# A written-out order of the first operations replaced by another, with other filler transposes

## The chip, the cores and the metric

The kernel runs on one core of a Trainium2 chip. Its time is the device time of one execution in microseconds; three runs before the change gave 608.42, 608.91 and 609.12, median 608.91. PE is the matrix engine, DVE the vector engine, ACT the scalar engine, POOL the general engine; SP issues nearly all DMAs. All five work from their own queues, strictly in order, and wait for each other by semaphores.

## What is computed

Lightning attention over 4 batches, 8 heads, 768 tokens and 64 columns a head, in blocks of 64 tokens with a running state, followed by two matrix products with a leaky ReLU between them:

```python
for b in range(nb):
    qb, kb, vb = (q[:, :, sl], k[:, :, sl], v[:, :, sl])
    intra = np.einsum('bhic,bhjc->bhij', qb, kb) * Dmask[None]
    intra = np.einsum('bhij,bhjd->bhid', intra, vb)
    inter = np.einsum('bhid,bhde->bhie', qb * lam_pow[None], kv_state)
    out[:, :, sl] = intra + inter
    kb_dec = kb * rev_pow[None]
    kv_state = lam_block[None, :, None, None] * kv_state + np.einsum('bhsd,bhse->bhde', kb_dec, vb)
...
x = attn_out.transpose(0, 2, 1, 3).reshape(B * S, H * D)      # 3072 x 512
h = x @ w_in                                                  # 512 x 2048, float64
g = np.maximum(0.01 * h, h)
return (g @ w_out).astype(np.float32)                         # 2048 x 512, float64
```

## The kernel before, in words

**Chunks and groups.** Tokens are taken in 24 chunks of 128 (two blocks of the reference at a time), six to a batch. Four chunks make a token group of 512; there are six groups. For every chunk PE transposes k and q (four 128x128 transposes each, line 546), forms the product of decayed k with v that updates the state ("k*v", line 410 in function kv), the scores (line 410 in go; DVE multiplies them by the mask, line 637), and the output of the chunk: first the own part, then two parts with the state (line 410 in own and inter). Between the two state parts a two-column copy (line 676) makes PE wait for the first to be written. Copies of the transposed k and q are line 527, the decay of k line 585, the scaled q line 592, the state update lines 642, 644 and 647.

**Splitting.** The products that follow need more than one pass's precision, so each operand is kept as three tiles: h (line 692 on ACT), l (line 700 on DVE) and m (line 718 on DVE) of the chunk's output x; and likewise wh, wl, wm of a weight slice (lines 806 or 808, 811, 817). Weights come as 64-bit floats, half a slice to a DMA (line 781), and are first turned into 32-bit floats by three ACT operations (793, 795, 797) and two DVE operations (799, 800).

**The first product, "up" (line 853).** For a group and one of eight weight slices, PE makes two blocks, each of four h, four l and four m matmuls into one PSUM bank; between l and m ACT scales the bank (line 878), and at the end ACT applies the leaky ReLU (line 881) and a DMA stores the block (884). Slices 1 of group 0 are done in two halves of two chunks, the 128x256 matmuls of the profile. An up of a group needs the h, l and m of all its chunks. The two buffers of x serve the groups in turn (group number modulo 2).

**The second product, "down" (line 920).** After all ups, from about 341 us on, PE does nothing but this until the end.

**What sets the order.** The program's operations are numbered as the code adds them, each with an engine (or several that could do it), a duration as its author guessed it, and what it reads and writes. The class Plan fixes their order in two stages (method emit). First comes the list ORDER, line 268, written out by hand or by a search: pairs of an operation's number and its engine. A negative number -n does not stand for an operation: it puts n filler transposes of the identity on PE (function busy, line 346, into a free PSUM bank), which compute nothing that is used. What the list leaves out is then placed by a greedy planner: of all operations that are able to run, the one that could start earliest by the guessed durations, ties by a rank that follows the list seq (line 961). The instructions are written out in the order that results; each engine, and SP's DMA queue, receives its own in that order. Nine more fillers come before everything (WARM). Which PSUM bank, raw buffer or store buffer an operation uses is also decided as it is placed.

The loads at the start that both orders move: k and q of a chunk are two DMAs of 128 KB each (line 466), v is one of 256 KB (line 524), half a weight slice one of 512 KB (line 781). Below, k0, q0, v0 stand for those of chunk 0, w10 and w11 for the halves of weight slice 1, w00 and w01 for those of slice 0. Before, SP's queue begins k0 q0 v0 w11 k1 v1 q1 k2 w10 q2 v2 k3 q3 v3 w01 w00.

Of the kernel before, what the change touches and what calls it, by code (L numbers as in the profile page):

```python
# [241 lines left out]
def kernel(  # L242
# [22 lines left out]
    T = GC * C  # L265
    WARM = 9
    LATER = 2.0
    ORDER = [(3, "DMA"), (4, "DMA"), (-6, "PE"), (6, "PE"), (8, "ACT"), (7, "PE"), (5, "DMA"), (9, "ACT"), (0, "DVE"), (1, "DVE"), (10, "POOL"), (13, "PE"), (2, "DVE"), (11, "DVE"), (15, "DVE"), (12, "PE"), (14, "DVE"), (-1, "PE"), (19, "PE"), (20, "PE"), (16, "POOL"), (17, "DVE"), (21, "DVE"), (101, "DMA"), (26, "DMA"), (29, "PE"), (33, "DVE"), (22, "PE"), (28, "DMA"), (36, "PE"), (18, "POOL"), (38, "DVE"), (39, "POOL"), (103, "ACT"), (23, "ACT"), (24, "DVE"), (27, "DMA"), (31, "ACT"), (102, "ACT"), (30, "PE"), (32, "ACT"), (-1, "PE"), (35, "PE"), (37, "DVE"), (40, "DVE"), (41, "POOL"), (34, "DVE"), (105, "DVE"), (49, "DMA"), (95, "DMA"), (96, "ACT"), (104, "ACT"), (52, "PE"), (56, "DVE"), (42, "PE"), (43, "PE"), (97, "ACT"), (50, "DMA"), (-1, "PE"), (53, "PE"), (98, "ACT"), (54, "ACT"), (55, "ACT"), (44, "DVE"), (25, "DVE"), (106, "DVE"), (99, "DVE"), (51, "DMA"), (-2, "PE"), (59, "PE"), (45, "PE"), (61, "DVE"), (100, "DVE"), (72, "DMA"), (73, "DMA"), (46, "ACT"), (75, "PE"), (107, "ACT"), (58, "PE"), (57, "DVE"), (47, "DVE"), (60, "DVE"), (76, "PE"), (155, "PE"), (74, "DMA"), (179, "DMA"), (78, "ACT"), (62, "POOL"), (79, "POOL"), (108, "DVE"), (63, "DVE"), (77, "ACT"), (173, "DMA"), (80, "DVE"), (48, "DVE"), (65, "PE"), (66, "PE"), (67, "ACT"), (-2, "PE"), (68, "PE"), (156, "PE"), (-1, "PE"), (81, "PE"), (180, "ACT"), (69, "ACT"), (70, "DVE"), (64, "POOL"), (84, "DVE"), (85, "POOL"), (181, "ACT"), (182, "ACT"), (174, "ACT"), (175, "ACT"), (82, "PE"), (83, "DVE"), (157, "PE"), (158, "PE"), (120, "DMA"), (111, "DMA"), (110, "DMA"), (119, "DMA"), (112, "DMA"), (88, "PE"), (89, "PE"), (114, "PE"), (159, "ACT"), (90, "ACT"), (91, "PE"), (176, "ACT"), (92, "ACT"), (183, "DVE"), (109, "DVE"), (160, "PE"), (123, "PE"), (86, "DVE"), (177, "DVE"), (184, "DVE"), (93, "DVE"), (178, "DVE"), (-1, "PE"), (164, "PE"), (113, "PE"), (165, "PE"), (161, "PE"), (217, "DMA"), (211, "DMA"), (136, "DMA"), (117, "DVE"), (116, "ACT"), (125, "ACT"), (115, "ACT"), (128, "PE"), (129, "PE"), (135, "DMA"), (121, "DMA"), (185, "ACT"), (71, "DVE"), (127, "DVE"), (186, "DVE"), (122, "PE"), (219, "ACT"), (124, "ACT"), (162, "ACT"), (166, "PE"), (241, "PE"), (167, "PE"), (242, "PE"), (138, "PE"), (87, "POOL"), (94, "DVE"), (118, "DVE"), (218, "ACT"), (213, "ACT"), (214, "ACT"), (212, "ACT"), (221, "DVE"), (131, "DVE"), (130, "DVE"), (-1, "PE"), (137, "PE"), (139, "PE"), (140, "PE"), (232, "DMA"), (132, "POOL"), (126, "DVE"), (133, "DVE"), (134, "POOL"), (220, "ACT"), (142, "PE"), (143, "PE"), (215, "DVE"), (222, "DVE"), (141, "ACT"), (243, "ACT"), (168, "ACT"), (144, "PE"), (145, "ACT"), (149, "ACT"), (148, "ACT"), (246, "PE"), (247, "PE"), (169, "PE"), (187, "DVE"), (216, "DVE"), (223, "ACT"), (244, "PE"), (170, "PE"), (234, "ACT"), (248, "ACT"), (151, "DVE"), (224, "DVE"), (153, "DVE"), (189, "DMA"), (226, "DMA"), (163, "DMA"), (188, "DMA"), (154, "DMA"), (275, "DMA"), (252, "PE"), (253, "PE"), (171, "ACT"), (233, "ACT"), (228, "ACT"), (227, "ACT"), (235, "ACT"), (249, "PE"), (191, "PE"), (152, "DVE"), (146, "DVE"), (190, "PE"), (150, "POOL"), (225, "DVE"), (229, "ACT"), (236, "DVE"), (230, "DVE"), (231, "DVE"), (192, "PE"), (193, "PE"), (194, "DVE"), (195, "PE"), (196, "PE"), (197, "PE"), (245, "ACT"), (202, "ACT"), (250, "ACT"), (237, "DVE"), (238, "DVE"), (206, "DVE"), (239, "DVE"), (254, "ACT"), (201, "ACT"), (277, "PE"), (320, "DMA"), (322, "ACT"), (288, "ACT"), (198, "ACT"), (321, "ACT"), (257, "PE"), (258, "PE"), (255, "PE"), (172, "DMA"), (326, "DMA"), (327, "ACT"), (204, "DVE"), (324, "DVE"), (207, "POOL"), (208, "DVE"), (203, "POOL"), (328, "ACT"), (259, "ACT"), (323, "ACT"), (330, "DVE"), (205, "DVE"), (199, "DVE"), (325, "DVE"), (329, "ACT"), (331, "DVE"), (332, "DVE"), (333, "DVE"), (268, "PE"), (269, "PE"), (263, "PE"), (256, "ACT"), (260, "PE"), (352, "DMA"), (274, "DMA"), (354, "ACT"), (210, "DMA"), (276, "PE"), (278, "PE"), (279, "PE"), (298, "DMA"), (281, "PE"), (282, "PE"), (355, "ACT"), (280, "ACT"), (261, "ACT"), (283, "PE"), (300, "PE"), (340, "PE"), (264, "PE"), (284, "ACT"), (311, "ACT"), (346, "DMA"), (251, "DMA"), (289, "POOL"), (209, "POOL"), (292, "DVE"), (293, "POOL"), (353, "ACT"), (265, "ACT"), (291, "DVE"), (446, "DVE"), (335, "PE"), (341, "PE"), (287, "ACT"), (348, "ACT"), (336, "PE"), (349, "ACT"), (270, "ACT"), (347, "ACT"), (356, "DVE"), (240, "DVE"), (266, "PE"), (267, "ACT"), (285, "DVE"), (271, "PE"), (272, "ACT"), (337, "ACT"), (296, "DMA"), (297, "DMA"), (299, "PE"), (301, "PE"), (302, "PE"), (303, "ACT"), (262, "DMA"), (411, "DMA"), (405, "DMA"), (294, "DVE"), (463, "DVE"), (334, "DVE"), (471, "DMA"), (458, "DMA"), (477, "DMA"), (455, "DMA"), (350, "DVE"), (357, "DVE"), (304, "PE"), (305, "PE"), (351, "DVE"), (306, "PE"), (338, "PE"), (358, "ACT"), (310, "ACT"), (307, "ACT"), (359, "DVE"), (308, "DVE"), (286, "DVE"), (309, "DVE"), (450, "DMA"), (273, "DMA"), (339, "ACT"), (342, "ACT"), (413, "ACT"), (407, "ACT"), (406, "ACT"), (388, "PE"), (361, "PE"), (343, "PE"), (362, "PE"), (344, "ACT"), (383, "PE"), (384, "PE"), (389, "PE"), (479, "DMA"), (454, "DMA"), (319, "DMA"), (470, "DMA"), (478, "DMA"), (447, "DMA"), (457, "DMA"), (366, "PE"), (367, "PE"), (360, "DVE"), (314, "DVE"), (200, "DVE"), (295, "POOL"), (412, "ACT"), (415, "DVE"), (147, "DVE"), (385, "ACT"), (390, "ACT"), (414, "ACT"), (408, "ACT"), (368, "ACT"), (391, "PE"), (386, "PE"), (369, "PE"), (468, "DMA"), (345, "DMA"), (472, "DMA"), (431, "DMA"), (437, "DMA"), (451, "DMA"), (464, "DMA"), (363, "ACT"), (364, "PE"), (365, "ACT"), (387, "ACT"), (370, "ACT"), (371, "DMA"), (459, "DMA"), (448, "DMA"), (449, "DMA"), (313, "POOL"), (290, "POOL"), (409, "DVE"), (315, "DVE"), (316, "POOL"), (317, "DVE"), (416, "DVE"), (494, "PE"), (495, "PE"), (312, "POOL"), (497, "PE"), (498, "PE"), (496, "DVE"), (499, "PE"), (410, "DVE"), (417, "DVE"), (461, "DMA"), (453, "DMA"), (462, "DMA"), (456, "DMA"), (503, "DVE"), (392, "ACT"), (452, "DMA"), (460, "DMA"), (393, "DMA"), (418, "DVE"), (432, "ACT"), (435, "DVE"), (433, "ACT"), (434, "ACT"), (436, "DVE"), (394, "PE"), (395, "PE"), (396, "ACT"), (439, "ACT"), (399, "PE"), (440, "ACT"), (372, "PE"), (425, "PE"), (373, "PE"), (438, "ACT"), (374, "ACT"), (465, "DMA"), (474, "DMA"), (400, "PE"), (401, "ACT"), (397, "PE"), (426, "PE"), (402, "PE"), (513, "DVE"), (441, "DVE"), (419, "DVE"), (442, "DVE"), (443, "DVE"), (510, "DVE"), (475, "DMA"), (398, "ACT"), (403, "ACT"), (512, "DMA"), (404, "DMA"), (480, "DVE"), (522, "DVE"), (377, "PE"), (375, "PE"), (376, "ACT"), (427, "ACT"), (555, "PE"), (378, "PE"), (379, "ACT"), (476, "DMA"), (469, "DMA"), (420, "PE"), (421, "PE"), (422, "ACT"), (380, "PE"), (556, "PE"), (381, "ACT"), (423, "PE"), (428, "PE"), (444, "DVE"), (467, "DMA"), (529, "DMA"), (473, "DMA"), (525, "DMA"), (561, "DMA"), (445, "DVE")]
    APART = 4
    FIRST_LOADS = ["k0", "q0", "v0", "k1", "q1", "v1", "w10", "k2", "q2", "v2", "w11", "k3", "q3", "v3"]  # L270
    LOW_PE, MIX_PE = set(), set()
# [772 lines left out]
```

## Time and profile before

| what | value |
|---|---|
| three runs, us | 608.42, 608.91, 609.12 |
| profiled execution: span from first to last instruction, us | 606.1 (its own total time is not shown; the median of the runs is 2.8 above the span) |
| PE busy, us and share of the span | 595.4, 98% |
| DVE, ACT, POOL busy, us | 308.5, 266.9, 73.4 |
| PE busy in 0 to 20 and 20 to 40 us | 14.74 and 18.10 |
| mean busy share of the DMA engines, 0 to 40 us | 92 to 93% |
| filler transposes (line 349) | 25: 9 at the start, 16 from the list |
| one 512-column matmul of line 853, start to start, four in a row | 0.91 us for four |

In rows of the timeline the first number is the start in us from the span's start, the second the length; then engine, line, operation, output and inputs, their shapes and how many were merged; in brackets how long the engine had been idle and what ended that. In the table by windows, each engine's busy time and number of instructions stand in the order PE, PEld (weight loads), DVE, ACT, POOL, then PE's granted clock, the DMA engines' busy share and GB/s. Where the text speaks of a landing, it is the last of the sixteen completions that the trace records for that DMA.

### The profile page before, as it was taken

What the parts mean: (1) busy time and instruction counts of PE and PEld (TensorE: products, weight loads), DVE (VectorE), ACT (ScalarE), POOL (GpSimd) and SP (SyncE); (2) the same over time, 40 slices, a digit from 0 to 9 for tenths busy, and PEclk for the clock granted to TensorE, in tenths of its full rate; (3) what the DMA queues carried; (4) which work ended last, traced back from release to release, by engine and by line L of the source; (5) the groups of instructions that cost most, each with busy time, mean ns of one, the idle gap of its engine ahead of it and who ended that gap; (6) DMA issues with size and microseconds to landing.
All of it is one profiled execution on the core that took longest, in us unless ns stands there. A gap on an engine that the chain in (4) does not pass through costs nothing.

```text
span 606.1 us, 12896 instructions
## 1 busy us (share of the span) xinstructions
PE 595.4 (98%) x5381; PEld 494.4 (82%) x5381; DVE 308.5 (51%) x425; ACT 266.9 (44%) x428; POOL 73.4 (12%) x83
## 2 busy tenths in 40 slices
PE   7899999999999999999999999999999999999997
PEld 5688888888888888888788888888888888888886
DVE  5888855334242344243467755455454544635531
ACT  3789865444555556565566432222312313214111
POOL 2232412214132023122000000000000000000000
PEclk9999999999999999999999999999999999999999
DMA  8998957676889878975775833423333333333201
GB/s 194 230 260 226 267 164 215 148 183 153 202 247 216 215 240 191 262 246 176 263 277 213 290 122 115 163 83 143 122 108 135 109 135 113 132 104 122 87 1 69
DMA packets 147754, 105.18 MB, mean 174 GB/s; under 512 B 123632, under 2 KB 124400, under 8 KB 147696
## 3 DMA queue, kind: packets, MB, share of 16 engines
q1 hardware_dynamic: 147408, 104.29, 58.1%
q8 instruction: 42, 0.69, 0.5%
q14 instruction: 16, 0.13, 0.1%
q10 hardware_dynamic: 288, 0.07, 0.0%
HBM read 68.69 MB, written 35.65 MB: 172 GB/s over the span
## 4 chain that ended last, share of the span: by engine, by line
PE 96%; SPq 2%; DMA 1%; issue 0%; DVE 0%; DVEq 0%; ACT 0%
PE b L853 33%; PE b L920 18%; PE pt L853 11%; PE po L920 11%; PE psc L920 11%; PE po L410 4%; PE pt L920 4%; PE psc L410 3%; SPq L466 2%; DMA gs<-in_k_dram 1%; PE b L546 1%; PE po L546 0%; SPq L781 0%; SPq L524 0%; PE pt L546 0%
## 5 line engine op out<-in xcount | busy, mean ns | idle before, releaser
L902 ACT ACTIVATE xh<-att 128x1024 fp32r<-128x1024 f32 x48 | 50.7, 1060 | 148.7 <-PE b L920 140.7
L903 DVE SCALAR_TENSOR_TENSOR xl<-att,xh 128x1024 fp32r<-128x1024 f32 x48 | 58.6, 1222 | 97.7 <-ACT xh L902 97.7
L853 PE MATMUL b<-xm,wm 128*128 128x512 f32 (+1 forms) x292 | 77.6, 391 | 0.0
L853 PE MATMUL b<-xh,wh 128*128 128x512 f32 (+1 forms) x292 | 77.4, 389 | 0.0
L853 PE MATMUL b<-xl,wl 128*128 128x512 f32 (+1 forms) x292 | 77.4, 388 | 0.0
L920 PE MATMUL b<-wh,xh 128*128 128x512 f32 x192 | 74.7, 389 | 0.0
L920 PE MATMUL b<-wl,xl 128*128 128x512 f32 x192 | 74.7, 389 | 0.0
L853 PEld LDWEIGHTS b<-xl,wl 128*128 128x128 f32 x292 | 54.2, 188 | 11.2
L853 PEld LDWEIGHTS b<-xh,wh 128*128 128x128 f32 x292 | 54.0, 188 | 11.1
L853 PEld LDWEIGHTS b<-xm,wm 128*128 128x128 f32 x292 | 53.5, 188 | 11.4 <-ACT b L878 0.3
L905 DVE SCALAR_TENSOR_TENSOR xm<-xl,xh 128x1024 fp32r<-128x1024 f32 x48 | 58.7, 1226 | 4.7
L878 ACT ACTIVATE b<-b 128x512 f32<-128x512 f32 x72 | 42.0, 586 | 34.8 <-PE b L853 34.8
L881 ACT ACTIVATE gs<-b 128x512 f32<-128x512 f32 x72 | 42.6, 597 | 30.3 <-PE b L853 24.3
L920 PEld LDWEIGHTS b<-wl,xl 128*128 128x128 f32 x192 | 36.0, 188 | 7.5
L920 PEld LDWEIGHTS b<-wh,xh 128*128 128x128 f32 x192 | 36.1, 188 | 7.4
L647 POOL TENSOR_TENSOR att<-att 128x256 f32<-128x256 f32 x40 | 30.9, 772 | 86.8 <-DVE att L644 73.9
L637 DVE TENSOR_TENSOR att<-psc,att 128x512 f32<-128x512 f32 x24 | 16.5, 689 | 45.4 <-PE psc L410 45.3
L920 PE MATMUL psc<-wm,xm 128*128 128x512 f32 (+1 forms) x100 | 37.9, 384 | 0.0
L799 DVE TENSOR_SCALAR w<-w 128x512 int32<-128x512 int32 x32 | 14.9, 468 | 44.1 <-ACT w L793 44.0
L920 PE MATMUL psc<-wh,xh 128*128 128x512 f32 x96 | 37.3, 389 | 0.0
L920 PE MATMUL psc<-wl,xl 128*128 128x512 f32 x96 | 37.3, 389 | 0.0
L920 PE MATMUL po<-wh,xh 128*128 128x512 f32 x96 | 37.3, 389 | 0.0
(98 smaller groups left out, 944.4 us busy)
## 6 DMA issues: line engine op xcount, KB each, us to landing
att<-g SPq DMA_DIRECT2D x48, 512.0 KB, 3.2
g<-gs SPq DMA_DIRECT2D x47, 512.0 KB, 3.6
raw<-in_moe_w_in_dram SPq DMA_DIRECT2D x16, 512.0 KB, 5.3
raw<-in_moe_w_out_dram SPq DMA_DIRECT2D x16, 512.0 KB, 4.6
out_dram<-gs SPq DMA_DIRECT2D x23, 256.0 KB, 2.1
att<-in_k_dram SPq DMA_DIRECT2D x44, 128.0 KB, 4.1
att<-in_v_dram SPq DMA_DIRECT2D x22, 256.0 KB, 4.1
wo<-w SPq DMA_DIRECT2D x8, 512.0 KB, 4.9
```

Of the source, the lines that this page charges most:

```text
L410: nc.tensor.matmul(dst[HALF[cols]], lhsT=lhsT[HALF[rows]], rhs=rhs[HALF[rows]], start=start, stop=True, skip_group_check=True)
L466: nc.sync.dma_start(out=dst[:, z * HP:(z + 1) * HP, :], in_=y[z::2].rearrange("h p d -> p h d"))
L637: add("DVE", 0.685, lambda: nc.vector.tensor_tensor(sc, psc[:, :, lower, :], decay, op=ALU.mult), ["psc", "fk"], ["sc"])
L647: add("POOL", 0.62, lambda new=new, j=j: nc.gpsimd.tensor_tensor(state[(j + 1) % 4], new, _bc(lam_c, 2, D), op=ALU.mult), [f"st{j % 4}", " ...
L799: add("DVE", 0.42, lambda: nc.vector.tensor_scalar(d, d, 3, None, op0=ALU.logical_shift_left), [], [key], lock=True)
L853: nc.tensor.matmul(dst, lhsT=w[z][:, kk * 2 * P + f * P:kk * 2 * P + (f + 1) * P], rhs=x[z][:, kk, toks], start=start and kk == 0, stop=kk ...
L878: add("ACT", ns, lambda b=b: nc.scalar.activation(out=b(), in_=b(), func=AF.Copy, bias=0.0, scale=S + 1.0), [], [kb], rank=-1.5)
L881: add("ACT", ns, lambda b=b, r=r: nc.scalar.activation(out=r(), in_=b(), func=AF.Prelu, bias=0.0, scale=1.0 / WS, alpha=0.01), [kb], [kg], ...
L902: add("ACT", 1.05, lambda: nc.scalar.activation(out=h, in_=graw[j], func=AF.Copy, bias=0.0, scale=NEAR), reads, wr("h"))
L903: add("DVE", 1.215, lambda: nc.vector.scalar_tensor_tensor(l, graw[j], 1.0, h.bitcast(F32), op0=ALU.mult, op1=ALU.subtract), reads + [f"rh ...
L905: add("DVE", 1.215, lambda: nc.vector.scalar_tensor_tensor(m, l.bitcast(F32), -S, h.bitcast(F32), op0=ALU.mult, op1=ALU.add), [f"rh{j}", f ...
L920: nc.tensor.matmul((to if z == 2 else acc[tb][0])[:, cols], lhsT=ring[j][z][:, f * T + tb * P:f * T + (tb + 1) * P], rhs=W[pp][z][:, f * d ...
```

## The change

One line is replaced: the list ORDER. The operations themselves are unchanged, and so are the nine fillers at the start.

- The list is shorter: 351 entries instead of 500. It names 348 operations and three groups of fillers; before it named 491 and nine groups. 347 operations stand in both; 144 are now left to the greedy planner, one is new in the list.
- The fillers of the list are 6, 14 and 6 instead of 6, 1, 1, 1, 2, 2, 1, 1 and 1. With the nine at the start PE executes 35 instead of 25. The 14 stand before the k*v product of chunk 0, the last 6 before chunk 0's own output.
- SP's queue begins q0 k0 w11 v0 w10 k1 q1 k2 q2 v1 v2 q3 k3 w00 v3 w01.
- Twelve operations of the list are on another engine: the copies of transposed k and q of chunk 0 (8 and 9) and of q of chunk 1 (32), two of the two-column copies of line 676 (90 and 141) and wh of a slice (223) on DVE instead of ACT; three more of the two-column copies (21, 44 and 194) on ACT instead of DVE; the decays of k 33, 56 and 126 on POOL instead of DVE.
- PE, DVE, ACT and POOL receive their operations in another order throughout the list, and so does what the planner adds behind it.

The diff, its one line wrapped here:

```diff
-    ORDER = [(3, "DMA"), (4, "DMA"), (-6, "PE"), (6, "PE"), (8, "ACT"), (7, "PE"), (5, "DMA"), (9, "ACT"), (0, "DVE"), (1, "DVE"),
-        (10, "POOL"), (13, "PE"), (2, "DVE"), (11, "DVE"), (15, "DVE"), (12, "PE"), (14, "DVE"), (-1, "PE"), (19, "PE"), (20, "PE"),
-        (16, "POOL"), (17, "DVE"), (21, "DVE"), (101, "DMA"), (26, "DMA"), (29, "PE"), (33, "DVE"), (22, "PE"), (28, "DMA"),
...
-        (428, "PE"), (444, "DVE"), (467, "DMA"), (529, "DMA"), (473, "DMA"), (525, "DMA"), (561, "DMA"), (445, "DVE")]
+    ORDER = [(4, "DMA"), (3, "DMA"), (101, "DMA"), (5, "DMA"), (0, "DVE"), (95, "DMA"), (1, "DVE"), (103, "ACT"), (-6, "PE"), (7, "PE"),
+        (26, "DMA"), (6, "PE"), (27, "DMA"), (10, "POOL"), (9, "DVE"), (2, "DVE"), (11, "DVE"), (-14, "PE"), (13, "PE"), (102, "ACT"),
+        (104, "ACT"), (49, "DMA"), (96, "ACT"), (8, "DVE"), (15, "DVE"), (105, "DVE"), (12, "PE"), (97, "ACT"), (50, "DMA"), (14, "DVE"),
+        (28, "DMA"), (16, "POOL"), (51, "DMA"), (73, "DMA"), (98, "ACT"), (-6, "PE"), (19, "PE"), (20, "PE"), (21, "ACT"), (29, "PE"),
...
+        (405, "DMA"), (465, "DMA"), (273, "DMA"), (466, "DMA"), (200, "DVE"), (355, "ACT"), (349, "ACT"), (262, "DMA")]
```

Operations 0 to 2 are the decay factors on DVE; 3 to 5 load k0, q0, v0; 6 and 7 transpose k0 and q0, 8 and 9 copy them; 10 decays k0; 12 is chunk 0's scores and 13 its k*v; 19 and 20 its own output and the first state part; 26 to 28 load k1, q1, v1; 49 to 51 load k2, q2, v2; 72 to 74 load k3, q3, v3; 95 and 101 load w10 and w11; 96 to 98 and 102 to 104 turn them into 32-bit floats on ACT.

## The prediction

> **What bounds the kernel now.** I read the page first, then the busy table by stage, then TensorE's own rows of the first 45 us, and last the rows around the one later place where the two orders differ in kind.
>
> ```profile
> PE 595.4 (98%) x5381; PEld 494.4 (82%) x5381; DVE 308.5 (51%) x425; ACT 266.9 (44%) x428; POOL 73.4 (12%) x83
> PE   7899999999999999999999999999999999999997
> ```
>
> ```profile
> 0.00:20.00 20.00, 14.74 (x318) 12.12 (x318) 12.26 (x36) 9.52 (x15) 4.36 (x12) 1.00 0.93 204
> 20.00:40.00 20.00, 18.10 (x407) 15.67 (x411) 18.10 (x31) 15.47 (x27) 4.81 (x7) 1.00 0.92 237
> 40.00:60.00 20.00, 20.00 (x384) 17.03 (x378) 16.54 (x27) 17.95 (x34) 7.53 (x6) 1.00 0.93 242
> ```
>
> The first number after each window's length is PE's busy time. PE lacks 5.26 us in the first window, 1.90 in the second and nothing from 40 to 280; behind 341 us (the second product) it is full to the end. DMA is 92 to 93% busy in all three windows. So the time is PE's fixed work plus what PE loses, and what a new order can win lies before 40 us: there the loads set the pace.
>
> ```profile
> 4.61 1.06 PE L546 MATMUL pt<-att 128*128 128x128 f32 x4
> 5.47 1.06 PE L546 MATMUL b<-att 128*128 128x128 f32 x4
> 7.59 0.69 PE L410 MATMUL b<-att 64*64 64x64 f32 x32 [1.07 <-DMA att<-in_v_dram]
> 9.56 0.93 PE L410 MATMUL po<-att 64*64 64x64 f32 x40 [0.55 <-DVE att L637]
> 11.86 0.69 PE L410 MATMUL b<-att 64*64 64x64 f32 x32 [0.41 <-DVE att L585]
> 13.12 0.81 PE L546 MATMUL b<-att 128*128 128x128 f32 x4 [0.56 <-DMA att<-in_q_dram]
> 14.60 0.69 PE L410 MATMUL psc<-att 64*64 64x64 f32 x32 [0.57 <-ACT att L527]
> 21.05 0.44 PE L546 MATMUL b<-att,gs 128*128 128x128 f32 x2 [1.30 <-DMA gs<-in_k_dram]
> 27.27 0.56 PE L410 MATMUL psc<-att 64*64 64x64 f32 x20 [0.85 <-issue]
> ```
>
> Start, length, work, and in brackets PE's idle time before it with what ended it. With two of 0.23 (at 16.11 and 17.04) the waits come to 5.8 us; 1.36 us of start-up are outside any order.
>
> ```profile
> 137.63 0.41 PE L410 MATMUL po<-att 64*64 64x64 f32 x16
> 137.97 1.19 PE L853 MATMUL b<-xm,wm 128*128 128x512 f32 x4
> 138.11 0.60 ACT L692 ACTIVATE xh<-po 128x512 fp32r<-128x512 f32 x1 [1.01 <-PE po L410]
> 139.01 1.08 PE L853 MATMUL pt<-xl,wl 128*128 128x512 f32 x4
> 139.18 0.65 DVE L700 TENSOR_TENSOR xl<-po,xh 128x512 fp32r<-128x512 f32 x1
> 139.93 1.07 PE L853 MATMUL b<-xh,wh 128*128 128x512 f32 x4
> ```
>
> This is the end of chunk 11, the last of token group 2 (chunks 8 to 11). PE's next group needs its xh and xl, which ACT and DVE make by 138.71 and 139.83. PE has two blocks of the older group in hand (137.97 and 139.01, 1.96 us) and loses nothing.
>
> **The sum's base.** The profiled span is 606.1; the page gives no time for what lies around it. The median of the runs is 608.91, so 2.8 us stand outside the span, and I add the change of the span to the median.
>
> **Part 1, the loads of the first 22 us.** SP's queue in the new program begins q0 k0 w11 v0 w10 k1 q1 k2 q2 v1 v2 q3 k3 w00 v3 w01 (k, q, v of a chunk; w = half of a weight slice); before it was k0 q0 v0 w11 k1 v1 q1 k2 w10 q2 v2 k3 q3 v3 w01 w00. Nothing is loaded that was not loaded, so wherever both queues have issued the same set, I take the same landing time. The trace's completions in the order before are: q0 5.7, v0 7.5, w11 9.0, k1 10.1, v1 11.3, q1 13.5, k2 14.3, w10 15.7, q2 17.1, v2 18.3, k3 21.0, q3 21.8, v3 22.6, w01 23.9, w00 25.4; successive completions are 1.3 to 1.6 us apart for a w, 0.8 to 1.8 for a v.
>
> - v0 now lands with w11 before it: the first four loads are the same set, so at 9.0 (7.5 before). PE is busy to 6.3 with the eight transposes; the 14 new fillers stand before the product k*v of chunk 0, which waits for v0. Eight transposes took 0.213 us each (1.06 at 4.61, from start to start); later ones 0.11 (0.44 for four at 38.47 in the chain). Two slow and twelve fast fillers end at 8.1: hidden, at nothing. If all are slow, 14 x 0.213 = 3.0 ends at 9.3 and costs 0.3. I take nothing.
> - By the Trainium skill (TensorE: Matmul & The Clock Gate, Part 1) the array starts at half rate, is released after about 3.4 us of activity, and the window runs free, so the point moves between runs; the trace agrees on the factor of two, though the slow spacing held here from 1.36 to 6.1 us. By that page alone the release could come later than 6.3 and the sum below would be +1.0 instead of +0.7.
> - The six next fillers (0.67) stand before chunk 0's output product, which waits for DVE's mask product: scores end about 10.1, DVE takes 0.69 (L637 at 8.81), so it starts near 11.0 and they are hidden as well. The old two fillers ahead of it stood in the same wait.
> - k1 and q1: against 13.5 the set has w10 for v1, so 13.8; k2 14.6, q2 15.7 to 16.0. v1 comes at 17.1 instead of 11.3, and PE stands there; v2 closes the set at 18.3, as before. Chunk 1's outputs, chunk 2's scores and chunk 2's k*v (0.5 us each by the x32 rows) end about 19.6; before, the same without chunk 2's scores (0.5) ended at 19.3.
> - q3 and k3 close their set at 21.8, PE has transposed both by about 22.0. Before, the same work was done at 22.46 (k3 at 21.05, then scores, then q3). Gain 0.5. Its bounds: a loss of 0.3, if the late completions (one of sixteen came 1.8 us behind the others for k3) fall on k3 again behind q3; a gain of 1.2 if they do not.
> - Moved between engines: three copies of a transposed k or q, two of chunk 0 (L527, 0.58 on ACT), go to DVE (nearest row there L637, 0.69), three decays of k (L585) from DVE (0.69) to POOL (1.06). They lie under the waits for v0 and v1: nothing. Should v0 come as early as before, the two copies of chunk 0 would add 0.2 (0.11 longer each).
>
> **Part 2, 22 to 48 us.** Here PE lost 0.85 (code, nothing the profile shows) and five fillers of 0.11: 1.4. The new queue has no filler past 12 us. It has these waits: chunk 3's output needs DVE's mask product, which now stands behind the splits of weights (L817 1.22, L811 1.22) and PE has only one block and k*v between: 0.6, bounds 0 and 1.2. k4 stands behind q4 and q5 in SP's queue; its set closes at 29.5 in the trace, PE comes to it at 28.8: 0.7, bounds 0 and 1.7 (one late completion, 1.8, less a little slack). v of chunk 5: 0.3, bounds 0 and 0.6. The code stall I let go in one bound and keep in the other. After: 1.6. Cost 0.2, bounds -1.4 and +3.
>
> **Part 3, the round of chunk 11.** The list written out ends earlier (351 entries against 500), and the planner fills the rest from another state. In the built queues this shows once: the two blocks that followed chunk 11 (an m and an l) now stand before its round, and the next instruction after chunk 11's last output product reads xh of chunk 11. From the rows: PE is free at 137.97, xh is there at 138.71 plus 0.06 (the usual step to a waiter: DVE ended 9.50, PE began 9.56): wait 0.80. Four h matmuls take 0.91 to 139.68; xl is done at 139.83 (DVE has L642 and a turn of 0.4 each before it, in the new order too): wait 0.2. Cost 1.0. The work put before it is not lost, PE does it earlier; only the cover is gone. Bounds 0.6 (DVE free at once, ACT as it was) and 1.3. What queues behind: the whole of the group's products on PE, so it is on the path.
>
> Elsewhere to 341 us PE finds the same blocks between chunks as before: nothing. The second product and the end are the same: nothing.
>
> Sum: -0.5 + 0.2 + 1.0 = +0.7; 608.9 + 0.7 = 609.6, and a span of 606.8.
>
> **Rivals.**
> *Faster, at 20 to 42 us.* All late loads come in time: the waits for k3 (1.30) and code (0.85) go, the five fillers (0.55) too, and none of the three new waits shows: -2.7; with chunk 11's 1.0 this is 607.2. For it: with both halves of w1 early the ups can fill PE. Against it: DMA is 92% busy there and the bytes are the same. It decides if k3 lands before about 20.5 and k4 before 28.8.
> *Slower: k4 and chunk 5 late.* The loads behind 25 us slip by one late completion, k4 waits 1.7, v5 0.6 and DVE's splits cost chunk 3 its 1.2, the code stall stays: part 2 is +3.0, the sum +3.5, 612.4; half of that gives 611. For it: DVE is 18.10 of 20 us busy in 20 to 40. It decides when part 2 exceeds +0.7, since the forecast then leaves 0.2%.
> *Chunk 11's hole closes.* If ACT or DVE come there with lag as planned, only parts 1 and 2 stay: 608.6.
>
> **How the numbers follow.** 0.2%, 1.2 us, is about what a measurement of this kernel can tell from no change. Forecast (609.6, within 608.4 to 610.2) 0.42; the slower rival, from 610.2 on, 0.37; the faster, below 607.7, 0.15; the closed hole 0.06. Within 0.2% are forecast and closed hole less the small part that lies outside: 0.46; slower 0.38; faster 0.16. The range goes from the faster rival to where 1 in 10 is left above: 607.2 to 612.0.
>
> **What would show it.** Right: chunk 0's first k*v near 9.1, no filler after 12 us, q3 and k3 transposed near 22, and between 130 and 145 us a wait of 0.8 for ACT's xh (L692) and 0.2 for DVE's xl (L700), where PE was full. Wrong: no such pair of waits, or PE waits before 48 us that sum to less than 4 or more than 9 us.

## The result and the profile after

The changed kernel takes 611.29 us (median of 15 runs, 609.50 to 614.69); the kernel before, on the same chip in between, 608.56 (15 runs, 607.27 to 609.19). The ratio is 1.0046, 95% interval 1.0030 to 1.0061, so 1.8 to 3.7 us slower. The number forecast was 609.6: the measured time is inside the range of 607.2 to 612.0 and on the side that was forecast, but 1.7 us above the number. The likeliest case ("Within 0.2%") did not come in.

The page of the changed kernel, busy times and PE in 40 slices:

```profile
PE 596.6 (98%) x5391; PEld 495.5 (82%) x5391; DVE 312.1 (51%) x426; ACT 263.6 (43%) x424; POOL 76.1 (13%) x86
PE   7799999999999999999999999999999999999997
```

The table by windows:

```profile
0.00:20.00 20.00, 16.01 (x349) 13.83 (x350) 13.96 (x36) 9.12 (x15) 6.54 (x14) 1.00 0.95 212
20.00:40.00 20.00, 17.36 (x365) 15.33 (x365) 16.11 (x27) 14.42 (x27) 8.18 (x8) 1.00 0.95 245
40.00:60.00 20.00, 19.77 (x414) 17.09 (x413) 18.48 (x30) 15.52 (x29) 5.35 (x6) 1.00 0.88 246
130.00:150.00 20.00, 19.28 (x306) 15.58 (x305) 7.32 (x19) 7.77 (x16) 7.00 (x8) 1.00 0.77 195
```

PE is busier in the first window (16.01 against 14.74; the fillers account for all of that: 35 of them, 6.03 us, against 20, 4.77 us), less busy in the second (17.36 against 18.10), and in the last two it has holes of 0.23 and 0.72 us where the kernel before was busy for all of the 20 us. PE's rows to 60 us, those with a wait and some others:

```profile
8.64 0.69 PE L410 MATMUL b<-att 64*64 64x64 f32 x32 [0.66 <-DMA att<-in_v_dram]
10.91 0.93 PE L410 MATMUL po<-att 64*64 64x64 f32 x40
14.18 0.44 PE L546 MATMUL b<-att,gs 128*128 128x128 f32 x2 [0.94 <-DMA gs<-in_k_dram]
16.64 0.24 PE L410 MATMUL pt<-att 64*64 64x64 f32 x1 [0.22 <-DMA att<-in_v_dram]
21.17 0.21 PE L410 MATMUL pt<-gs 64*64 64x64 f32 x1 [1.75 <-issue]
21.56 0.66 PE L546 MATMUL b<-att,raw 128*128 128x128 f32 x4
22.05 0.60 PE L546 MATMUL b<-att,gs 128*128 128x128 f32 x4
26.84 0.64 PE L410 MATMUL b<-gs 64*64 64x64 f32 x29 [1.46 <-issue]
56.42 0.27 PE L410 MATMUL po<-att 64*64 64x64 f32 x2 [0.23 <-issue]
```

Of the waits that the prediction put between 22 and 48 us (mask product, k4, v of chunk 5) none is there. Instead PE stands three times, from 19.4 us on, for "issue", which is time in which it waited for nothing that the profile shows: 1.75 us in the middle of chunk 2's k*v, 1.46 at the start of chunk 3's, 0.23 at 56 us. The kernel before had one such row, 0.85.

The end of chunk 11, PE, ACT and DVE:

```profile
140.58 0.41 PE L410 MATMUL po<-att 64*64 64x64 f32 x16
141.06 0.60 ACT L692 ACTIVATE xh<-po 128x512 fp32r<-128x512 f32 x1
141.71 1.20 PE L853 MATMUL b<-xh,wh 128*128 128x512 f32 x4 [0.72 <-ACT xh L692]
142.12 0.65 DVE L700 TENSOR_TENSOR xl<-po,xh 128x512 fp32r<-128x512 f32 x1
142.83 1.19 PE L853 MATMUL b<-xl,wl 128*128 128x512 f32 x4
```

This is the forecast pair: h waits for ACT's xh, and l begins 1.12 us after h (0.91 in a row that waits for nothing), just behind xl.

**Where the time went.** Both programs run the same matmuls of line 853 in nearly the same order, so the start of the n-th one, minus its start in the trace of before, shows how far a trace lags. At four places (their times in the trace of before), in us:

| kernel (one profiled execution each) | 90.6 | 133.1 | 148.4 | 335.9 |
|---|---|---|---|---|
| changed | 0.17 | 0.17 | 1.21 | 1.80 |
| changed, again | 5.41 | 5.41 | 6.45 | 6.57 |
| without 14 fillers | -0.12 | -0.12 | 0.92 | 1.11 |
| 64 PE instructions more | 9.40 | 9.40 | 10.46 | 10.46 |
| block behind chunk 11 | 1.22 | 1.22 | 1.33 | 1.53 |
| both (two executions) | 0.47, -0.64 | 0.47, -0.65 | 0.54, -0.54 | 0.53, -0.54 |
| old loads | 7.66 | 7.66 | 8.75 | 8.75 |
| old loads, w10's steps later | 1.22 | 1.22 | 2.28 | 2.28 |

The step between 133 and 148 us is chunk 11: 1.04 to 1.09 us in each program that has the wait of 0.72 there, 0.07 to 0.11 in each where the block was moved back. Nearly all the rest arises before 85 us, and there two executions of one and the same program differ by 5.24 us. So one profile does not tell what the start costs; the runs do, by their medians.

### The profile page after: what moved, and what is told of

Same layout as the page of the kernel before. It is cut to its first block, busy times and chain, and to the rows that moved or that the text cites. A ratio compares the mean times of both kernels' runs of the same rounds, so it can differ in the third digit from the quotient of the medians.

```text
span 607.9 us, 12932 instructions
## 1 busy us (share of the span) xinstructions
PE 596.6 (98%) x5391; PEld 495.5 (82%) x5391; DVE 312.1 (51%) x426; ACT 263.6 (43%) x424; POOL 76.1 (13%) x86
## 4 chain that ended last, share of the span: by engine, by line
PE 93%; SPq 3%; DMA 2%; issue 1%; ACT 1%; DVE 0%; POOL 0%; DVEq 0%
PE b L853 31%; PE b L920 18%; PE po L920 11%; PE psc L920 11%; PE pt L853 10%; PE po L410 4%; PE pt L920 4%; PE psc L410 3%; SPq L466 1%; DMA raw<-in_moe_w_out_dram 1%; DMA att<-in_v_dram 1%; SPq L509 1%; PE po L546 0%; SPq L524 0%; PE pt L546 0%
## 5 line engine op out<-in xcount | busy, mean ns | idle before, releaser
L920 PE MATMUL po<-wl,xl 128*128 128x512 f32 x96 | 37.3, 389 | 0.0
L920 PE MATMUL po<-wm,xm 128*128 128x512 f32 x96 | 37.3, 389 | 0.0
L920 PE MATMUL b<-wm,xm 128*128 128x512 f32 x96 | 37.3, 389 | 0.0
```

The costliest lines, as they stand in the source:

```text
L920: nc.tensor.matmul((to if z == 2 else acc[tb][0])[:, cols], lhsT=ring[j][z][:, f * T + tb * P:f * T + (tb + 1) * P], rhs=W[pp][z][:, f * d ...
```

## The experiments

Ratios are to the kernel before, run in between on the same chip; each median is of 12 runs, those of "64 PE instructions more" and "old loads" of 6. The edits below are given by what they do, not letter for letter. They add lines to the kernel, so that L410 of the changed kernel is L414 to L421 in their rows, and the other lines shift alike.

| kernel | median, before's median (us) | ratio, 95% interval |
|---|---|---|
| changed, again | 610.73, 609.25 | 1.0035 (1.0016 to 1.0054) |
| without 14 fillers | 609.33, 609.25 | 1.0010 (0.9992 to 1.0028) |
| 64 PE instructions more | 614.42, 609.25 | 1.0087 (1.0055 to 1.0118) |
| block behind chunk 11 | 609.70, 609.25 | 1.0004 (0.9985 to 1.0023) |
| both | 608.30, 608.87 | 0.9984 (0.9962 to 1.0005) |
| both, again | 608.85, 609.02 | 1.0003 (0.9987 to 1.0019) |
| block behind chunk 11, 7 small products for the fillers | 609.91, 609.02 | 1.0019 (1.0004 to 1.0034) |
| the same with 57 | 609.77, 609.02 | 1.0020 (1.0001 to 1.0039) |
| before, 32 PE instructions more | 608.98, 608.87 | 0.9995 (0.9974 to 1.0016) |
| before, without its last 9 fillers | 609.21, 608.87 | 1.0003 (0.9982 to 1.0025) |
| old loads | 615.40, 608.87 | 1.0090 (1.0061 to 1.0118) |
| old loads, w10's steps later | 612.25, 608.95 | 1.0053 (1.0030 to 1.0076) |

### The same program again

No edit.

> The changed kernel once more, unchanged. Its trace showed two idle times of PE that nothing in the profile ends (1.75 us inside chunk 2's k*v at 21.17, 1.46 us ahead of chunk 3's k*v at 26.84), and its times went with the granted clock (1.000: 609.5 to 610.9; 0.994: 612.3 to 614.7). Theory 'code': the idle times are PE's program arriving in loads of 256 instructions, so they stand at the same two instructions in any execution (number 705 and 961 of PE's records), 1.4 to 2.0 us each. Theory 'clock': in some executions the clock falls back for a stretch of some 3.5 us, and the time is 1.7 us longer for each such stretch; a trace with a clock of 0.997 or 0.994 would show transposes or 512-column matmuls at twice their spacing somewhere before 40 us. Rival 'chance': idle times wander by more than 0.5 us between executions. Time expected 611 (609.5 to 613).

Its profiled execution was a long one, span 612.7. PE's stops again, then the count of PE's instructions up to a moment inside each stop, first here and then in the first trace of the changed kernel:

```profile
22.96 0.21 PE L410 MATMUL pt<-gs 64*64 64x64 f32 x1 [2.57 <-issue]
60.02 0.27 PE L410 MATMUL po<-att 64*64 64x64 f32 x2 [2.01 <-issue]
```

```profile
0.00:22.90 22.90, 15.82 (x349) 13.62 (x350) 13.13 (x36) 9.10 (x15) 6.57 (x14) 1.00 0.90 210
0.00:59.90 59.90, 50.73 (x1109) 44.28 (x1110) 45.88 (x88) 35.96 (x63) 18.77 (x27) 0.97 0.90 224
```

```profile
0.00:21.10 21.10, 16.01 (x349) 13.83 (x350) 13.96 (x36) 9.14 (x15) 6.54 (x14) 1.00 0.96 218
0.00:26.80 26.80, 20.23 (x475) 17.70 (x476) 18.31 (x43) 12.97 (x23) 9.78 (x17) 1.00 0.97 223
0.00:56.35 56.35, 49.55 (x1109) 43.30 (x1110) 44.94 (x87) 35.65 (x63) 19.45 (x27) 1.00 0.92 231
```

After the window's bounds and length come PE's busy time with its matmuls (x349) and PEld's with its weight loads (x350). PE stops after 349 matmuls and 350 loads in both, and after 1109 and 1110 in both; 475 and 476 lie one step of 126 behind the first, 1109 about six such steps. The places are fixed by the count; how long PE stands there (1.75 or 2.57, 1.46 or nothing, 0.23 or 2.01) is not, so the expected "1.4 to 2.0 each" fell. The code hypothesis gives the step a meaning: the queue that the page calls "instruction" (q8) moved 42 packets of 16 KB (0.69 MB), and the 10,782 PE and PEld instructions of the page make 257 to a packet, near the step of 126 matmuls and 126 weight loads (the place in PE's program where one packet ends and the next begins is called a boundary below):

```profile
q8 instruction: 42, 0.69, 0.5%
```
In the first trace its second packet ran from 18.04 to 19.61 us and the stop ended at 21.17; the third from 24.14 to 25.40, and the stop ended at 26.84; the eighth from 54.01 to 54.97, and the stop ended at 56.42. The kernel with 57 products below, which has 200 PE instructions more, moved 43 packets instead of 42.

The kernel before stood at the same count in its one "issue" row, in quite other work:

```profile
0.00:27.20 27.20, 20.10 (x475) 16.52 (x476) 18.46 (x45) 14.79 (x25) 7.35 (x16) 1.00 0.93 214
```

The clock: the same execution in stretches of 3.4 us; the third number from the end is the granted clock.

```profile
19.90:23.30 3.40, 0.83 (x44) 0.67 (x36) 0.69 (x2) 1.09 (x2) 0.62 (x1) 1.00 1.07 298
23.30:26.70 3.40, 3.40 (x40) 3.13 (x38) 3.13 (x5) 1.17 (x2) 1.89 (x2) 0.50 1.09 252
26.70:30.10 3.40, 3.26 (x160) 2.91 (x160) 2.02 (x4) 2.74 (x6) 0.76 (x2) 1.00 0.79 176
57.45:60.85 3.40, 1.39 (x43) 1.14 (x36) 3.33 (x5) 1.48 (x4) 0.00 (x0) 1.00 0.87 222
60.85:64.26 3.41, 3.41 (x10) 2.64 (x9) 2.08 (x4) 2.81 (x6) 0.62 (x1) 0.50 0.87 273
```

A stop that leaves PE 0.83 or 1.39 us of work in such a stretch is followed by 3.4 us at half clock; the stop is paid a second time. By the Trainium skill (TensorE: Matmul & The Clock Gate, Part 1) the window is free-running, 3413 ns long, and the clock falls back after an idle one; the stretches here are 3.41 us long, as it says, but the window ahead of each was not idle.

### Without the 14 fillers

```diff
-            busy(14)     # ahead of chunk 0's k*v
+            busy(0)
```

> The changed kernel without the 14 fillers that stand before chunk 0's k*v; every other instruction of every queue is the same. By the prediction they are hidden under the wait for v0, so chunk 0's k*v still starts at 8.6 to 9.1 and the time stays within 0.3 us. Theory 'code': 28 PE instructions fewer stand before everything, so the boundaries at 705 and 961 fall 28 instructions later in the program; the first idle time moves into the last outputs of that stretch or the transposes of q3, 14 quads on, and the sum of the two changes by -1.2 to +0.3. Theory 'clock': PE is idle 1.6 us longer in the first 9 us, so the clock is released later or falls back more often: +1.7 in some executions, matmul spacings double somewhere after 8 us.

1.4 us less than the changed kernel beside it (609.33 against 610.73). PE now waits for v0 for 2.87 us, and k*v starts at 9.64:

```profile
9.64 1.13 PE L415 MATMUL b<-att 64*64 64x64 f32 x32 [2.87 <-DMA att<-in_v_dram]
22.95 0.66 PE L551 MATMUL b<-att,raw 128*128 128x128 f32 x4 [2.16 <-DVE xl L705]
```

The expectation of 8.6 to 9.1 was missed, since v0 came later in this execution, and the clock was at half speed from 7.8 to 14.6 us; yet the time fell. (Line numbers are 5 higher here: L551 is L546.) The first stop has moved 14 products on, from the middle of chunk 2's k*v to the transposes of q3 behind it, as expected for 28 instructions fewer. The row names DVE's xl, but that was done at 22.01, 0.9 us before PE went on, and the count is the old one, 349 matmuls and 349 loads at 22.8 us; q3 had landed at 19.65, and the code packet ended at 21.72. The second stop is gone. In 7 of the 12 executions the mean granted clock was 0.994 or less, in the changed kernel beside it in 2 of 12: the clock was lower more often without the fillers, and yet the kernel was not slower. So the fillers' time is hidden, as predicted; that what they cost is the place of the boundaries is tried below with other instructions in their stead.

### 64 PE instructions more

```diff
             busy(14)
+            for i in range(16):
+                quad(bank[at][:, 0:C2], 0, ident[:, 0:C2], ident[:, 0:C2], i % 2, True)
```

> The changed kernel with 64 more PE instructions: 16 products of 64x64 (the quads of k*v, on the identity, unused) behind the 14 fillers, under the same wait for v0 (0.47 us of work in a wait that still has 0.66). Nothing else changes. Theory 'code': all boundaries of 256 instructions now fall 64 instructions earlier in the program: no idle time in chunk 2's k*v at its ninth quad any more, but one in the outputs of chunk 1 or scores of chunk 2 that stand 64 instructions before it, the second one likewise before chunk 3's k*v, and, as a boundary comes into the quads near 28 and near 47 us, one or two idle times more there: sum +1.2 to +2.4 us. Rival 'data' (the two idle times are late loads or another engine's step that the profile fails to name): they stay at the same two instructions with the same 1.75 and 1.46 us, and the time stays within 0.3 us.

+3.7 us on the changed kernel beside it (expected +1.2 to +2.4; the rival 0.3 at most). Each stop moved in the program and stayed in the count:

```profile
20.46 0.39 PE L415 MATMUL po<-att 64*64 64x64 f32 x11 [1.62 <-issue]
27.02 0.58 PE L415 MATMUL psc<-att 64*64 64x64 f32 x10 [2.95 <-issue]
54.53 0.70 PE L415 MATMUL po<-att 64*64 64x64 f32 x16 [2.74 <-issue]
```

```profile
0.00:20.40 20.40, 16.34 (x350) 14.13 (x350) 14.01 (x36) 8.82 (x14) 6.56 (x14) 1.00 0.92 214
0.00:26.90 26.90, 19.95 (x476) 17.40 (x476) 17.13 (x41) 11.25 (x19) 9.80 (x17) 1.00 0.94 221
0.00:54.40 54.40, 44.71 (x983) 39.27 (x984) 38.01 (x76) 30.27 (x52) 16.00 (x23) 0.93 0.88 219
```

350, 476, and 983 (five steps behind the first). Nothing else in any queue was changed, so "late data" falls; that the stops are PE's program arriving late is what remains, and it is the queue of code whose packets end 1.4 us ahead of the end of each of the three (19.03, 25.60 and 53.13). From about the end of the second and third stop the clock was at half speed for 6.8 us each; that this is why the time rose by more than expected is not shown.

### The block behind chunk 11

```diff
+        # the planned order: the m block 703 behind chunk 11's last output (632), its leaky ReLU 704 behind xh (633)
+        for x, behind in ((703, 632), (704, 633)):
+            move(x, behind)
```

> The changed kernel with one m block (four 512-column matmuls, 0.91 us) and its leaky ReLU moved from before the round of chunk 11 to behind it, as the kernel before has such blocks there. All other order is kept. By the prediction PE's wait of 0.72 for xh (L692) and the rest for xl at 141 us close: -0.7 to -0.9 us against the changed kernel. Rival: the wait only moves to where the moved block's successor stands (its leaky ReLU now comes behind xh on ACT, so a bank comes free later): 0 to -0.3.

```profile
140.66 0.41 PE L414 MATMUL po<-att 64*64 64x64 f32 x16
141.01 1.19 PE L857 MATMUL b<-xm,wm 128*128 128x512 f32 x4
142.04 1.08 PE L857 MATMUL b<-xh,wh 128*128 128x512 f32 x4
142.96 1.15 PE L857 MATMUL b<-xl,wl 128*128 128x512 f32 x4
```

The wait is gone, and nothing came in its place: 609.70 against 610.73 beside it, and the step in the table of lags is 0.11 instead of 1.04.

### Both together

The two edits above.

> The changed kernel without the 14 fillers and with the m block behind the round of chunk 11. If the two gains (-1.4 and -1.0 us against the changed kernel) are of separate causes, they add: about 608.3 us, and equal to the kernel before within 0.2%. If the one without fillers was chance of the clock, 609.3 to 609.7 as with either alone.

> The changed kernel without the 14 fillers and with the m block moved, once more beside the two others. Expected 608.3 (607.8 to 608.8), against the kernel before -0.3 to +0.1%: its idle time at record 705 is there in each trace (2.4 us), the one at 961 is not.

608.30 and, once more, 608.85: ratios 0.9984 and 1.0003. Within the noise the gains add. Without these two the new order is as fast as the old, and not measurably faster. Both traces still have one stop, at 349 matmuls, of 2.42 and 1.89 us, where the kernel before loses 0.85 at its own; every trace of the new order has such a stop of 1.5 us or more, so what the order would be worth without one is not known.

### Code without fillers, and the same boundaries another way

```diff
-            busy(14)
+            for i in range(7):     # second kernel: 57
+                quad(bank[at][:, 0:C2], 0, ident[:, 0:C2], ident[:, 0:C2], i % 2, True)
```

> The changed kernel with the m block behind chunk 11's round and, in place of the 14 fillers (28 PE instructions, 1.5 us), seven unused 64x64 products (28 PE instructions, 0.2 us), all under the wait for v0. So PE's program has its boundaries where the changed kernel has them, without the fillers' time and activity. Theory 'code': what the fillers cost is the place of the boundaries: the time stays at that of the kernel with fillers and the block moved, 609.7 (609.2 to 610.4), idle times at records 705 and 961. Rival 'fillers' (their time, or the clock): 608.3 as without fillers.

> The same with 57 such products (228 PE instructions, 1.7 us of work, about as long as the 14 fillers). As 228 is 256 less 28, the boundaries fall where the kernel without fillers has them, one load earlier in the program, while PE is as busy as with fillers. Theory 'code': 608.3 (607.6 to 608.9), one idle time at the record that answers to 705 of the kernel without fillers (now 961), little or none at the next. Rival 'fillers': 609.7 as with them.

With seven small products, as many instructions as the 14 fillers in an eighth of the time, the stops are back where the fillers had put them, and so is the time (609.91; with fillers 609.70, without either 608.85 beside it):

```profile
21.10 0.21 PE L419 MATMUL pt<-gs 64*64 64x64 f32 x1 [1.52 <-issue]
26.50 0.64 PE L419 MATMUL b<-gs 64*64 64x64 f32 x29 [1.18 <-POOL att L656]
56.59 0.27 PE L419 MATMUL po<-att 64*64 64x64 f32 x2 [0.75 <-issue]
```

The middle row names POOL, but POOL had been done for 1.0 us, and the row stands at 475 matmuls and 476 loads too. So it is the number of instructions and not the fillers' work that places the stops. What that place costs is less sharp. The step from 608.85 to 609.91 alone is within its intervals; with the two other pairs (610.73 to 609.33, 609.70 to 608.30) it has one sign and 1.1 to 1.4 us each time. The second pair was run on two chips, on which the kernel before took 609.25 and 608.87, and is 1.0 by the differences to it. The mean of the three, taken from means of the runs, is 1.1 us with a 95% interval of 0.5 to 1.7.

The kernel with 57 does not test what its expectation says. Its 228 instructions are 28 short of a whole step against the kernel without fillers, so its boundaries do not fall where that has them but 28 instructions further on. It stopped for 2.14 and 1.43 us there, 609.77. Besides, its products and chunk 0's k*v kept PE to 12.29 us, where the changed kernel is done with k*v at 9.33. Its time is the one that the rival forecast (609.7), but with the boundaries in a third place it shows no more than that this place is no better.

### The kernel before, 32 instructions more

```diff
             busy(1)      # ahead of chunk 0's own output
+            for i in range(8):
+                quad(bank[at][:, 0:C2], 0, ident[:, 0:C2], ident[:, 0:C2], i % 2, True)
```

> The kernel before with 32 more PE instructions: eight 64x64 products on the identity, unused, behind the one filler that stands under the wait of chunk 0's output for DVE's mask product (0.55 us of wait, 0.24 us of work). Nothing else changes. Theory 'code': boundaries of PE's program fall 32 instructions earlier in the program; the one at record 1985, which PE passed at 53.40 with a load that came just in time, then lies in front of the quads at 50 us, and the stretch of 256 instructions ahead of it is run through in some 3 us less: a new idle time of 1 to 3 us there, and the sum is +1 to +2.5 us against the kernel before. Rival 'data or order': +0 (within 0.3 us), no idle time at 50 us.

Missed: no change, and no stop at 50 us. PE ran from the step that ends at 48.5 us to the next in 2.1 us, where other stretches of some 5 us were too short; but the packet for the end of that stretch had been under way since 48.14, before PE reached even its beginning. So the request went out ahead of what PE executed, and the expectation had counted from the boundary. Long matmuls filled PE there (up to 47.9 us); that this is why it went out early enough is likely, not shown.

### The kernel before, without its last nine fillers

```diff
-            busy(n)
+            busy(n if calls < 4 else 0)
```

> The kernel before without its last nine fillers (those from 13.8 us on). By the prediction five of them, from 22 to 48 us, cost PE 0.55 us, the others lie under waits: -0.55. Theory 'code': besides, boundaries fall up to 18 instructions later in the program, which by the passing times should change the idle times by -0.5 to +0.2: together -0.3 to -1.0. Rival 'clock': fillers keep the clock from falling back; without them some executions lose 1.7 us more: 0 to +1.

No change, 1.0003 (0.9982 to 1.0025). Both the 0.55 us that the prediction booked as a gain for fillers left out and the -0.3 to -1.0 expected here are not to be seen. In its one trace PE lost 1.2 us from 40 to 60 us, where the kernel before lost nothing, and the clock was at half speed from 13.2 to 20.0 us; so whether the gain was never there or was lost again is open.

### The old loads

```diff
-        SP: q0 k0 w11 v0 w10 k1 q1 k2 q2 v1 v2 q3 k3 w00 v3 w01
+        SP: k0 q0 v0 w11 k1 v1 q1 k2 w10 q2 v2 k3 q3 v3 w01 w00
```

> The changed kernel with SP's first sixteen loads in the order of the kernel before (k0 q0 v0 w11 k1 v1 q1 k2 w10 q2 v2 k3 q3 v3 w01 w00); the two ACT steps on w10 go behind it, all other queues are the changed kernel's. By the prediction the new load order with its PE order gains 0.5 by 22 us; with the old loads chunk 1's k*v comes at 14 to 15 instead of 16.6, but k3 and q3 are not there before 21.0 and 21.8 and the 14 fillers end after v0: +0.1 to +0.5 us. Theory 'code': PE reaches instruction 705 earlier or later with its loads, but the idle time there ends with the code load, some 5 us after instruction 449 was passed; if 449 is passed 1 us earlier, the idle time ends earlier too: -0.5 to +0.5 us. If the load order were what costs the change its 2.7 us: -1.5 us or more.

Missed by far: some 4.7 us on the changed kernel (+0.1 to +0.5 expected). ACT's queue of the new order has w10's three steps ahead of chunk 0's two-column copy (line 676, here 686), and with the old loads w10 lands at 16:

```profile
16.13 0.66 ACT L803 ACTIVATE w<-raw 128x512 f32<-128x512 f32 x1 [4.74 <-DMA raw<-in_moe_w_in_dram]
16.69 0.76 ACT L805 ACTIVATE low<-raw 128x512 uint16<-128x512 uint32 x1
17.32 0.75 ACT L807 ACTIVATE low<-raw 128x512 f16<-128x512 f32 x1
17.94 0.13 ACT L686 COPY att<-po 128x2 f32<-128x2 f32 x1
```

```profile
18.14 0.66 PE L420 MATMUL po<-att 64*64 64x64 f32 x8 [4.28 <-ACT att L686]
```

The last run therefore also moved these three steps, and DVE's three on w10, behind the work of chunk 1.

> The changed kernel with SP's first sixteen loads in the old order, and with the three ACT and three DVE steps that turn w10 into 32-bit floats moved behind the work of chunk 1 on their engines (as the kernel before has them), so that nothing of chunks 0 and 1 is queued behind that late load. PE's and POOL's queues are the changed kernel's. In the run that moved the loads alone, PE lost 4.3 us to a two-column copy on ACT that was queued behind w10's steps. If that was all, the 4.5 us go. By the prediction's first part the new loads gain 0.5 us: 611.2 (610.7 to 611.8) here. Theory 'code': PE gets past record 449 by 16 to 17 as in the changed kernel, and the idle time at record 705 is there again (1.5 to 2.8 us). Rival 'the loads cost the change its time': 609.5 or less.

612.25, above the 610.7 to 611.8 expected and far from the rival's 609.5; ratio 1.0053, against 1.0046 and 1.0035 for the changed kernel with its own loads. The 4.3 us wait is gone, and the stop at 349 matmuls is there again (1.97 us). The new loads, with the order of w10's steps that goes with them, are worth 0.4 to 1.1 us by these ratios; the intervals overlap, so the sign is likely, not shown. The loads are not what costs the change its time.

## Why the prediction was right or wrong

**The whole.** The measured time lies in the range and on the side that was forecast. Part 3 earned that; the rest is in part luck, since the range left room for three late waits that did not come, and stops of another kind took that room.

**The base.** The prediction put 2.8 us outside the span. The changed kernel's profiled execution took 609.72 with a span of 607.9: 1.8 outside. So the trace of before was of an execution about 1 us below its median. Adding a difference of spans to a median then assumes that the start is alike in all executions, and it is not.

**Part 1, -0.5.** Single steps held: k*v of chunk 0 at 8.64 (9.1 expected), own output at 10.91 ("near 11.0"), chunk 1's k*v at 16.64 (17.1). Then "chunk 2's k*v ... end about 19.6" failed: PE stopped in the middle of it from 19.42 to 21.17. q3 and k3 were transposed by 22.41 instead of 22.0, and before by 22.46: nothing gained. Not all of the 1.75 us is a loss, for k3's last completion came at 21.09 in this trace too. That the new loads help, with the right size, agrees with the last run.

**The 14 fillers, "hidden, at nothing".** Their time is hidden. The failed step is that an instruction hidden under a wait costs nothing: 28 more instructions moved the boundaries of PE's program into the 64x64 products of chunks 2 and 3, and this costs about 1 us (1.0 to 1.4 in three pairs of medians). Had the prediction asked which instruction of the new queue stands at the count of the old 0.85 us stop, it would have found chunk 3's k*v and, a step earlier, chunk 2's.

**Part 2, +0.2.** This is the step that failed most: "The code stall I let go in one bound and keep in the other. After: 1.6." The 1.6 was made of three waits for DVE and two loads, and none of them appeared in the trace; the stall, seen as one accident of 0.85 us, has a place that follows from counting. In the changed kernel it stands up to three times: 1.75, 1.46, 0.23 in one execution, 2.57, none, 2.01 in another, the second also with two falls of the clock. Over the runs parts 1 and 2 together cost 0.4 to 1.7 us (1.5 and 2.7 in all, less 1.04), not -0.3.

**Part 3, +1.0.** Right: 1.04 to 1.09 in every trace that has the order, 0.72 of it a named wait, and moving one block back took it away.

**Elsewhere to 341 us, at nothing.** Right but for one execution: the first trace lost 0.6 more between 245 and 275 us, the others 0 to 0.2.

**The rivals.** "Slower: k4 and chunk 5 late" has the right size (611 at half its price) and the wrong mechanism; in the trace PE waited for neither k4 nor chunk 5. "Faster" needed the code stall to go, and the new order made it longer. The test "PE waits before 48 us that sum to less than 4 or more than 9" could not have caught this: they sum to 5.3, against 5.8 before, a like sum from other waits.

**Open.** Why a packet of code comes 4 us after the boundary in one execution and 6 in the next, and how far ahead PE asks for it, was not settled. The DMA engines are 95% busy there, and the packets of the changed kernel took 0.9 to 1.6 us; a run with fewer bytes in that stretch was not made.

## What to carry to other kernels

Where an engine stands for "issue" (or for an engine that had long been done), count its instructions up to there in two kernels: counts that are equal, or whole packets apart, where the work is not, point to a program that comes late. Then any instruction ahead, hidden or not, can move the stop, and a dense run of short ones can bring one; the kernel before took 32 more at no cost. When a planner's list is cut short, look at each place where a group's last result is read next: one block of matmuls moved across it was worth 1 us here. And take the effect on a start-up that depends on loads from medians: one profile each can be 5 us apart with nothing changed.

## What the runs showed of the hardware

- PE's program comes in packets of 16 KB, one for about 126 matmuls with their 126 weight loads. From passing one boundary to running behind the next took 4.0 to 6.6 us wherever PE had to wait (17.1 to 21.10 with the seven small products, 16.9 to 21.17 and 21.17 to 26.84 in the changed kernel; 20.46 to 27.02 and 48.2 to 54.53 with 64 instructions more). The 64x64 products run through a packet in 2.3 us (16.9 to 19.2).
- In every trace here PE's first instruction behind such a stop came 1.2 to 1.7 us after the packet's end. A last completion of a data load around it can be late as well: k3's at 21.09 in the changed kernel, 1.0 us after the fifteenth.
- Stretches at half clock are 3.4 or 6.8 us long. The 3.4 us ahead of one held 0.83 and 1.39 us of PE's work in the changed kernel's second trace, 0.80 and 1.22 with 64 instructions more, and 1.61 with the block behind chunk 11 (18.51 to 21.93). No bound comes out of the traces: with 57 products 1.68 us (23.12 to 26.53) brought no fall, and 2.05 (29.95 to 33.36) did. Over 27 runs of the changed kernel those with a mean clock of 0.999 or more took 610.2 in the mean (8 runs), those of 0.994 or less 613.2 (6). The kernel before has such runs too (608.6 in 52 of 104 runs, 610.3 in 15). So the clock widens both; at full clock the changed kernel is still 1.6 us slower, and the clock is only a part of the difference.
